# Linear attention and a gated two-layer network in one kernel: key-value products moved from the first layer to the rows of the batch before

## The chip, the cores and the metric

The kernel runs on one core of one Trainium2 chip. The core has TensorE (PE, matrix products into the PSUM banks), VectorE (DVE), ScalarE (ACT), GpSimd (POOL) and SyncE (SP). Each engine runs its own queue of instructions in order; semaphores make one wait for another. SP and POOL are used here mostly to issue DMA transfers. The metric is the device time of one execution in microseconds, lower is better. Times of single instructions come from one execution that was profiled.

## The reference

For 8 batches of 8 heads, 576 positions and a head size of 64, a linear attention without softmax is followed by a root-mean-square norm, and a two-layer network with a gate is applied to the 4608 rows of 512 numbers that come out:

```python
kv = np.einsum('bhsd,bhse->bhde', k, v)
out = np.einsum('bhsd,bhde->bhse', q, kv)
rms = np.sqrt(np.mean(out * out, axis=-1, keepdims=True) + 1e-06)
x = (out / rms * g_norm)            # per batch, then rows of 8 heads x 64
h = x @ w_in                        # 512 -> 2048
g = h * (1.0 / (1.0 + np.exp(-1.702 * h)))
y = g @ w_out                       # 2048 -> 512
```

Inputs and output are float32. The kernel computes in float16 with float32 sums.

## The kernel before

The program is written out by Python code, with the order of every engine's instructions given by hand. The network works on tiles of 512 rows. The first 512 positions of each batch make one tile, and the last 64 positions of all eight batches make a ninth, so the outer loop has steps t = 0 to 8. Step t runs both layers of tile t on TensorE, and between their products it places the attention of batch b = t + 1.

**The two layers.** For t of 1 and over, each layer is computed with seven products of half-size blocks instead of eight. The *first layer* (`hid_seven`, `SevenIn.product`, L559) is a list of 28 products in the string of a `Plan`, each of four TensorE instructions over 256 columns: "21" is product 1 of part 2. A word "kv" in that string is a place without a product, at which the key-value products of the next batch are hung. The copies that hold intermediate results (`snap`, L509) and the gates (L539) go to ScalarE or VectorE as the plan says. The *second layer* (`Seven.run`, L681) is 112 instructions of 256 columns, numbered n = 0 to 111: products 1, 5, 6, 2, 7, 3, 4 with 16 steps each. Other work is hung on a number with `at2(n, ...)` and stands behind the n-th instruction. A `Plan`'s `ready` and `later` say at which places VectorE forms the sums `gS` (L611) that products 5, 6, 7 and 3 read; an entry (4, 8, 1) forms rows 4 to 7 of sum 1. One product of the first layer ("34") is late: it stands behind step 15.

**The attention of batch b** (class `Attention`, batches 2 to 7) has these pieces:

- `load_kv`, `load_q` (L114 to L140): POOL issues the loads of k, v and q of the first 512 positions, and of the rest of 64 positions. There is one buffer for k and one for v (`kraw`, `vbuf`), so a load waits until the products before have read them. There are two for q.
- `kv_all` (L238): for each pair of heads ten small products k'v, 40 in all, into one PSUM tile `kvp`; then four copies (`keep_kv`) move it into `kvd`, of which there are two that alternate by batch.
- `transpose_q` (L273, L275): SP issues transposing DMAs of q.
- `rows` (L313): q times `kvd`, 32 small products for half of the rows; ScalarE squares both halves (`sq`, L323, three buffers).
- `add_up` (L329), `roots` (L338), `turn` (L341): VectorE sums the squares per head, ScalarE takes the inverse root, VectorE multiplies; SP transposes the result with two DMAs into `xT`, which is the next tile of the network.
- `out`, `ss`, `apply` (L287, L358, L374): the same norm for the 64 positions of the rest.

In step t = 2 to 6 (plan `LATER`) the key-value products of batch t + 1 stand in the first layer as its third word, the loads of batch t + 2 behind its 15th, and `rows` behind step 15 of the second layer, both halves at once, right behind the late product. Step t = 1 uses the plan `SECOND`, with "kv" as its 22nd word and `rows` behind step 19. The allocation of a PSUM tile picks a free bank of its pool: `ps_a` and `ps_h` hold three banks each, `ps_o` two.

Of the kernel before, what the change touches and what calls it, by code (L numbers as in the profile page):

```python
# [7 lines left out]
F16 = mybir.dt.float16  # L8
# [4 lines left out]
P = 128  # L13
# [3 lines left out]
def kernel(  # L17
# [10 lines left out]
    nc = tc.nc  # L28

    B, H, S, D = q.shape  # L30
    DM = H * D
    DFF = moe_w_in.shape[1]
    NPAIR = H // 2
    FO = DFF // P
    KO = DM // P
    EPS = 1e-6
    SM = 512
    J = SM // P
# [10 lines left out]
    const = ctx.enter_context(tc.tile_pool(name="const", bufs=1))  # L49
    stage = ctx.enter_context(tc.tile_pool(name="stage", bufs=4))  # L50
    attn = ctx.enter_context(tc.tile_pool(name="attn", bufs=4))
# [18 lines left out]
    ident = const.tile([P, P], F16)  # L70
    ones2 = const.tile([P, P], F16)
    eps_t = const.tile([P, 1], F32)
    g_col = const.tile([P, 1], F32)
    w_in_sb = const.tile([P, KO, DFF], F16)
    w_out_sb = const.tile([P, FO, DM], F16)
# [32 lines left out]
    RW = J * D  # L108
    RS = H * RW

    def load_kv(b, h0=0, h1=H, rest=True):

        for n in "kv":
            nc.gpsimd.dma_start(  # L114
                out=kv_rows[n][:, h0 * RW : h1 * RW].rearrange("p (h x) -> p h x", x=RW),
                in_=srcs[n][b, h0:h1, 0:SM, :].rearrange("h (p j) d -> p h (j d)", j=J),
            )
        for n in "kv" if rest else "":
            nc.gpsimd.dma_start(
                out=kv_rows[n][0:R, RS : RS + H * D].rearrange("p (h d) -> p h d", d=D),  # L120
                in_=srcs[n][b, :, SM:S, :].rearrange("h p d -> p h d"),
            )

    def clear_rest():
        for n in "kv":
            nc.vector.memset(kv_rows[n][R:P, RS : RS + H * D], 0.0)
# [19 lines left out]
    for n in "kqv":  # L146
        if n != "q":
            rows = stage.tile([P, 6, 2 * P], F32, name="qf", tag="qf", bufs=2)
            rows = rows.rearrange("p h x -> p (h x)")[0:PE_]
# [8 lines left out]
        out=ident,  # L158
        in_=ident,
# [42 lines left out]
    xT = {}  # L202
# [8 lines left out]
    class Attention:  # L211
# [3 lines left out]
        def __init__(self, b):  # L215
            self.b, self.kb = b, kvb[b] if b < EARLY else kvd[b % 2]
            self.qT, self.o = {}, {}
            x = xpool.tile([P, KO * SM], F16, name="xT", tag="xT")
            if b < EARLY:
                self.x = xT[b] = x.rearrange("p (c n) -> p c n", c=KO)  # L220
            else:
                self.x = x.rearrange("p (m r) -> p m r", r=P)
                xT[b] = x.rearrange("p (j c r) -> p c j r", j=J, c=KO)
                self.x16 = attn.tile([P, J, DM], F16, name="x16", tag="x16", bufs=1)

        def kv(self, c):
            if c % self.KEEP == 0:
# [35 lines left out]
        def keep_kv(self, c0, c1):  # L263

            for half in range(2):
                to = slice(half * D, (half + 1) * D)
                for hl in range(2):
                    r = slice(hl * D, (hl + 1) * D)
                    copy(self.engine, self.kb[to, c0:c1, half, 1 - hl], self.kvp[r, c0:c1, :])

        def transpose_q(self):
            self.qTd = attn.tile([P, H * J // 2, P], F16, name="qTd", tag="qTd", bufs=1)
# [16 lines left out]
        def out(self, c):  # L289
            pool, tag = (ps_a, "att") if c < NPAIR else self.rest_pool  # L290
            t = pool.tile([P, SM], F32, name="outT", tag=tag)
            if c < NPAIR:
                n = SM
                self.product(t, c)
            else:
                n = NPAIR * R
                for i in range(NPAIR):
                    self.rest_product(t[:, i * R : (i + 1) * R], i)
            t = t[:, 0:n]
            sq = attn.tile([P, SM], F16, name="sq", tag="sq", bufs=3)  # L300
            nc.scalar.activation(sq[:, 0:n], t, AFT.Square)
            self.o[c] = (t, sq, n)

        def rows(self, i):

            t = [
                pool.tile([P, DM], F32, name="outR", tag=tag)
                for pool, tag in ROW_BANKS[i]
            ]
            for h in range(H):  # L310
                for half in range(2):
                    r = slice(half * D, (half + 1) * D)
                    nc.tensor.matmul(  # L313
                        t[half][:, h * D : (h + 1) * D],
                        self.qTd[r, h * (J // 2) + i, :],
                        self.kb[r, h // 2, half, 1 - h % 2, :],
                        start=(h == 0),
                        stop=True,
                        skip_group_check=True,
                    )  # L320
            for half in range(2):
                sq = attn.tile([P, SM], F16, name="sq", tag="sq", bufs=3)
                nc.scalar.activation(sq, t[half], AFT.Square)  # L323
                self.o[2 * i + half] = (t[half], sq)

# [12 lines left out]
            nc.scalar.activation(s4, s4, AFT.Abs_reciprocal_sqrt, bias=eps_t, scale=1.0 / D)  # L338

        def turn(self, j):  # L340
            nc.vector.tensor_mul(  # L341
                self.x16[:, j, :].rearrange("p (h d) -> p h d", d=D),
                self.o[j][0].rearrange("p (h d) -> p h d", d=D),
                self.sum4[:, j, :].unsqueeze(2).to_broadcast([P, H, D]),
            )
            if j % 2:
                nc.sync.dma_start_transpose(
                    out=self.x[:, (j - 1) * KO : (j + 1) * KO, :],
                    in_=self.x16[:, j - 1 : j + 1, :].rearrange("p j n -> p (j n)"),
                )  # L350
# [157 lines left out]
    def copy(engine, to, src):  # L508
        (nc.vector.tensor_copy if engine == "D" else nc.scalar.copy)(to, src)  # L509
# [347 lines left out]
    for hl in range(2):  # L857
        r = slice(hl * D, (hl + 1) * D)
# [34 lines left out]
    for fo in COLS[4:GROUP]:  # L893
# [28 lines left out]
        {'rows': (19, 19), 'add_up': (22, 26, 27, 31), 'table': 26, 'roots': (27, 33), 'turn': (40, 50, 51, 52)},  # L922
    )
    LATER = Plan(
# [4 lines left out]
        {1: 'DAAA', 5: 'AAAD'},  # L929
        "D",  # L930
        "aooa",
        "aahh",
        {15: '34'},
        (0, 1, 6, 11),
        {'rows': (15, 15), 'add_up': (17, 20, 24, 28), 'table': 24, 'roots': (28, 39), 'turn': (35, 38, 46, 48)},
    )
    LAST_TWO = Plan(
# [12 lines left out]
    def plan(t):  # L950
        return SECOND if t < EARLY else LATER if t < B - 1 else LAST_TWO
# [7 lines left out]
    for t in range(NT):  # L959
        b = t + 1  # L960
        u1, u2 = {}, {}

        def at1(i, f, *args):
            u1.setdefault(i, []).append(lambda: f(*args))

        def at2(i, f, *args):
            u2.setdefault(i, []).append(lambda: f(*args))  # L967

        def of(b, name, *args):
            return lambda: getattr(live[b], name)(*args)  # L970

        if t == 0:
# [25 lines left out]
            at2(39, load_kv, 2, 0, H // 2, False)  # L998
            at2(51, clear_rest)
            at2(51, load_kv, 2, H // 2, H)  # L1000

            def first_sum():
# [3 lines left out]
            at2(55, first_sum)  # L1006
        elif b < B:
            todo = plan(t)
            at1(todo.steps.index("kv"), of(b, "kv_all", todo.keep))
            if t == 1:  # L1010
                at1(5, start, b)
                at1(5, of(b, "transpose_q"))
                at1(4, nc.scalar.preload_act_table_set, "gelu_apprx_sigmoid_and_others")
                for n, i in ((1, 8), (2, 11), (3, 16)):
                    at1(i, weight_sum, n, 6, HF)
            if t + 2 < B:
                late = max(15, todo.steps.index("kv") + 1)
                at1(late, load_kv, t + 2)
                at1(late, load_q, t + 2)
                at2(100, start, t + 2)  # L1020
                at2(100, of(t + 2, "transpose_q"))
            at = todo.attn
            at2(at["table"], nc.scalar.preload_act_table_set, "abs_reciprocal_sqrt_and_small")
            for h in range(2):
                at2(at["roots"][h], of(b, "roots", h))
            for j in range(J):
                if j < J // 2:
                    at2(at["rows"][j], of(b, "rows", j))
                for name in ("add_up", "turn"):
                    at2(at[name][j], of(b, name, j))  # L1030
            at2(46, of(b, "out", NPAIR))
            at2(74, of(b, "ss", NPAIR))
            at2(80, of(b, "apply", NPAIR))
            at2(82, nc.scalar.preload_act_table_set, "gelu_apprx_sigmoid_and_others")
        elif t < B:
            for name in ("ss_pool", "rest_pool"):
                at2(16, setattr, live[1], name, (ps_a, "att"))
            at2(16, of(1, "out", NPAIR))
            at2(34, nc.scalar.preload_act_table_set, "abs_reciprocal_sqrt_and_small")
            at2(44, of(1, "ss", NPAIR))  # L1040
            at2(50, of(1, "apply", NPAIR))
            at2(52, nc.scalar.preload_act_table_set, "gelu_apprx_sigmoid_and_others")
# [31 lines left out]
```

## Time and profile before

| | |
|---|---|
| median of 3 runs | 259.46 us (258.91 to 261.26) |
| the profiled execution | 259.37 us |
| its span, first to last instruction | 257.6 us |
| busy: PE, DVE, ACT, POOL | 250.6, 195.0, 174.9, 55.0 us |
| clock granted to TensorE | 1.00 |
| kvp products (L238), 240 instructions | 4.9 us busy |
| copies of kvp (L509, VectorE, 64x256), 24 | 10.1 us busy |
| moved by DMA | 35.33 MB, mean 137 GB/s |

Busy times of one engine overlap those of another, so they don't add up to the span. A row of a timeline gives the start in us from the first instruction, the length, the engine, the line of the kernel, the operation, and "out<-in" with the shape (partitions x elements). Several instructions of one kind that follow each other are one row with "x" and their number. In brackets stands how long the engine was idle ahead of it and what ended the wait.

### The profile page before, as it was taken

The numbers are of one execution on the slowest core, as the hardware profiler recorded it, in microseconds if no ns is written. First come the engines' busy times: TensorE is split into PE (matmuls) and PEld (weight loads), VectorE is DVE, ScalarE is ACT, GpSimd is POOL, SyncE is SP. The second block draws the span as 40 slices with busy tenths as digits, with TensorE's granted clock in tenths as the row PEclk, the third lists the DMA queues.
The fourth block names the chain that finished last, engine by engine and source line by source line (L and its number), as shares of the span: only waits on it lengthen the run. The fifth ranks groups of instructions, "written<-read, shape, count | busy, mean of one in ns | idle before, by whom it ended". The sixth has DMA issues, their size and how long they took to land.

```text
span 257.6 us, 6353 instructions
## 1 busy us (share of the span) xinstructions
PE 250.6 (97%) x2596; PEld 203.3 (79%) x2596; DVE 195.0 (76%) x351; ACT 174.9 (68%) x315; POOL 55.0 (21%) x83
## 2 busy tenths in 40 slices
PE   7889999999999999999999999999999999999993
PEld 2434554788888888888888888888888888888883
DVE  1655677899968896889689968996899687557842
ACT  3477825988749974997499748984798569737820
POOL 8963245117025002500160007000000000000011
PEclk9999999999999999999999999999999999999999
DMA  7999999999989947996799479948600430012005
GB/s 170 200 202 206 204 204 197 230 200 138 161 194 170 215 59 151 154 213 90 172 147 223 62 177 138 229 58 178 159 4 0 93 154 3 0 79 88 3 21 142
DMA packets 68607, 35.33 MB, mean 137 GB/s; under 512 B 37922, under 2 KB 66082, under 8 KB 68322
## 3 DMA queue, kind: packets, MB, share of 16 engines
q0 software_dynamic: 37552, 18.17, 55.1%
q1 hardware_dynamic: 30624, 16.36, 27.9%
q8 instruction: 20, 0.33, 0.5%
q10 hardware_dynamic: 402, 0.39, 0.5%
q14 instruction: 9, 0.07, 0.1%
HBM read 36.70 MB, written 9.44 MB: 179 GB/s over the span
## 4 chain that ended last, share of the span: by engine, by line
PE 92%; POOL 3%; DMA 3%; issue 0%; DVE 0%
PE o L681 38%; PE h L559 38%; PE o L795 5%; PE hT L452 5%; DMA w_in_sb<-in_moe_w_in_dram 3%; PE kvp L238 2%; PE outR L313 1%; POOL kraw L90 1%; POOL qraw L90 1%; PE ss L358 1%; POOL vbuf L90 1%; POOL w_in_sb L171 0%; PE q L433 0%; PE kvp L250 0%; PE outT L283 0%; PE outT L287 0%
## 5 line engine op out<-in xcount | busy, mean ns | idle before, releaser
L539 ACT ACTIVATE gT<-h 128x512 f16<-128x512 f32 x96 | 52.5, 602 | 5.4 <-PE h L559 5.4
L559 PEld LDWEIGHTS <-ws 128*128 128x128 f16 x512 | 50.1, 98 | 5.9
L681 PEld LDWEIGHTS <-gS 128*128 128x128 f16 x512 | 49.4, 98 | 6.2 <-DVE gS L611 0.3
L559 PE MATMUL h<-xS,ws 128*128 128x256 f16 x384 | 52.2, 273 | 0.0
L681 PE MATMUL o<-tw,gS 128*128 128x256 f16 x384 | 46.5, 273 | 0.0
L681 PEld LDWEIGHTS <-gT 128*128 128x128 f16 x384 | 37.5, 98 | 4.3
L559 PEld LDWEIGHTS <-w_in_sb 128*128 128x128 f16 x384 | 37.1, 98 | 4.7
L559 PE MATMUL h<-xT,w_in_sb 128*128 128x256 f16 x224 | 31.9, 273 | 0.0
L681 PE MATMUL o<-w_out_sb,gT 128*128 128x256 f16 x256 | 31.4, 273 | 0.0
L573 DVE TENSOR_TENSOR h<-h,s 128x512 f32<-128x512 f32 x32 | 22.2, 697 | 6.8 <-PE h L559 5.5
L114 POOL DMA_DIRECT2D kraw<-in_k_dram x7 | 6.0, 853 | 91.0 <-PE kvp L238 86.5
L575 DVE TENSOR_TENSOR s<-h,s 128x512 f32<-128x512 f32 x32 | 22.1, 691 | 4.1 <-PE h L559 3.3
L656 DVE TENSOR_TENSOR osb<-o,qf 128x512 f32<-128x512 f32 (+1 forms) x25 | 16.7, 667 | 11.2 <-PE o L681 8.3
L611 DVE TENSOR_TENSOR gS<-gT 128x512 f16<-128x512 f16 (+2 forms) x32 | 21.2, 684 | 0.6 <-ACT gT L539 0.6
L539 ACT ACTIVATE gT<-s 128x512 f16<-128x512 f32 x32 | 19.9, 628 | 2.6 <-DVE s L575 2.6
L714 POOL DMA_DIRECT2D out_dram<-osb x4 | 2.2, 546 | 90.9 <-DVE osb L656 90.9
L559 PE MATMUL h<-xS,w_in_sb 128*128 128x256 f16 x128 | 18.9, 273 | 0.0
L360 ACT ACTIVATE rs<-ss,eps_t 128x512 f32<-128x512 f32 (+1 forms) x16 | 9.2, 581 | 13.7 <-PE ss L358 13.6
L967 ACT ACT_TABLE_LOAD x14 | 18.0, 1283 | 0.2
L648 ACT COPY qf<-o 128x512 f32<-128x512 f32 (+1 forms) x26 | 14.2, 546 | 4.5 <-PE o L681 4.4
L329 DVE TENSOR_REDUCE sum<-sq 128x8 f32<-128x512 f16 x24 | 15.3, 680 | 2.5 <-ACT sq L323 2.5
L509 ACT COPY h<-h 128x512 f32<-128x512 f32 x27 | 15.7, 586 | 2.1 <-PE h L559 2.0
(100 smaller groups left out, 361.9 us busy)
## 6 DMA issues: line engine op xcount, KB each, us to landing
out_dram<-osb SPq DMA_DIRECT2D x8, 512.0 KB, 4.2
kraw<-in_k_dram POOLq DMA_DIRECT2D x5, 512.0 KB, 9.2
vbuf<-in_v_dram POOLq DMA_DIRECT2D x5, 512.0 KB, 12.1
out_dram<-osb SPq DMA_DIRECT2D x2, 1024.0 KB, 4.9
qraw<-in_q_dram POOLq DMA_DIRECT2D x3, 512.0 KB, 13.4
qbuf<-in_q_dram POOLq DMA_DIRECT2D x3, 512.0 KB, 13.3
out_dram<-osb SPq DMA_DIRECT2D x6, 192.0 KB, 5.5
w_in_sb<-in_moe_w_in_dram POOLq DMA_DIRECT2D x2, 512.0 KB, 10.7
```

The costliest lines, as they stand in the source:

```text
L329: nc.vector.tensor_reduce(out=self.sum4[:, j, :], in_=self.o[j][1].rearrange("p (x d) -> p x d", d=D), op=ALU.add, axis=mybir.AxisListType.X,)
L452: nc.tensor.matmul(self.h[fo], w_in_sb[:, ko, fo * P : (fo + 1) * P], self.x[:, ko], start=(ko == 0), stop=(ko == KO - 1),)
L509: (nc.vector.tensor_copy if engine == "D" else nc.scalar.copy)(to, src)
L539: nc.scalar.activation(self.gT[:, to, n * TH : (n + 1) * TH], src, AFT.Gelu_apprx_sigmoid)
L559: nc.tensor.matmul(bank[name][:, a], w, x, start=(p in (1, 5) and a == 0 and k == 0), stop=(k == KH - 1), skip_group_check=True,)
L573: nc.vector.tensor_add(bank["z"], bank["x"], self.s5)
L575: nc.vector.tensor_add(self.s5, bank["x"], self.s5)
L611: op(s[:, n, lo], a, b)
L648: nc.scalar.copy(self.kept[as_][:, m], ps)
L656: nc.vector.tensor_add(o, ps, self.kept[with_][:, m])
L681: nc.tensor.matmul(o, a, w, start=(p in (1, 2, 5) and i == 0 and (mo == 0 or split)), stop=(i == HF - 1), skip_group_check=True,)
L967: u2.setdefault(i, []).append(lambda: f(*args))
```

## The change

1. For t = 1 the products of batch 2 stay in the first layer. Those of batch 3 go to step 95 of the second layer, with the copies on VectorE, ScalarE, VectorE, ScalarE ("DADA"), and the loads of batch 4 follow behind step 96.
2. For t = 2 to 5 the products of batch t + 2 stand behind step 15 of the second layer, right ahead of `rows` of batch t + 1, with the copies on ScalarE, VectorE, ScalarE, VectorE ("ADAD"). So the products of batches 4 to 7 come a step earlier than `rows` of the same batch. The word "kv" leaves the plan `LATER`, whose first products change order.
3. For t = 2 to 4 the load of k of batch t + 3 follows these products. The loads of v, of the rests and of q stand behind step 101, and behind a POOL copy of one element (`mark`) out of `xT[b]`, so that POOL waits there until the transposed rows of batch t + 1 have landed.
4. `x16` is allocated in the first `turn` and no longer when a batch starts; there are four buffers `sq` instead of three.
5. `ss`, `apply` and the table load of the second layer go from steps 74, 80, 82 to 82, 88, 90. In `LATER`, sum (4, 8, 3) goes from step 22 to 29, and the sums `ready` and `xsums` follow the shorter list.

```diff
-    def load_kv(b, h0=0, h1=H, rest=True):
-
-        for n in "kv":
+    def load_kv(b, h0=0, h1=H, rest=True, main="kv"):
+
+        for n in main:
...
+    def after_turn(b):
+
+        nc.gpsimd.tensor_copy(out=mark, in_=xT[b].rearrange("p c j r -> p j c r")[0:1, J - 1, KO - 1, 0:1])
...
-                    copy(self.engine, self.kb[to, c0:c1, half, 1 - hl], self.kvp[r, c0:c1, :])
+                    copy(
+                        self.engine[2 * half + hl],
+                        self.kb[to, c0:c1, half, 1 - hl],
+                        self.kvp[r, c0:c1, :],
+                    )
...
-            sq = attn.tile([P, SM], F16, name="sq", tag="sq", bufs=3)
+            sq = attn.tile([P, SM], F16, name="sq", tag="sq", bufs=4)
...
         def turn(self, j):
+            if j == 0:
+                self.x16 = attn.tile([P, J, DM], F16, name="x16", tag="x16", bufs=1)
...
     LATER = Plan(
-        "21 01 kv 22 05 25 06 11 02 15 26 03 16 12"
+        "21 01 25 22 05 06 11 02 15 26 03 16 12"
         " 07 31 27 13 17 35 36 04 23 24 32 33 14 37",
-        {23: ((0, 4, 0), (0, 4, 1)), 26: ((4, 6, 0),)},
-        {0: ((0, 8, 2),), 16: ((4, 8, 1),), 22: ((4, 8, 3),), 58: ((0, 4, 3),)},
+        {22: ((0, 4, 0), (0, 4, 1)), 25: ((4, 6, 0),)},
+        {0: ((0, 8, 2),), 16: ((4, 8, 1),), 29: ((4, 8, 3),), 58: ((0, 4, 3),)},
...
-        (0, 1, 6, 11),
+        (0, 1, 5, 10),
...
         elif b < B:
             todo = plan(t)
-            at1(todo.steps.index("kv"), of(b, "kv_all", todo.keep))
+            at = todo.attn
             if t == 1:
+                at1(todo.steps.index("kv"), of(b, "kv_all", "DDDD"))
...
+                at1(22, load_kv, 3)
+                at1(22, load_q, 3)
+                at2(95, start, 3)
+                at2(95, of(3, "kv_all", "DADA"))
+                at2(96, load_kv, 4)
+                at2(96, load_q, 4)
+            elif t + 2 < B:
+                at2(at["rows"][0], start, t + 2)
+                at2(at["rows"][0], of(t + 2, "kv_all", "ADAD"))
+                if t + 3 < B:
+                    at2(at["rows"][0], load_kv, t + 3, 0, H, False, "k")
+                    at2(101, after_turn, b)
+                    at2(101, load_kv, t + 3, 0, H, True, "v")
+                    at2(101, load_q, t + 3)
             if t + 2 < B:
-                late = max(15, todo.steps.index("kv") + 1)
-                at1(late, load_kv, t + 2)
-                at1(late, load_q, t + 2)
-                at2(100, start, t + 2)
                 at2(100, of(t + 2, "transpose_q"))
...
-            at2(74, of(b, "ss", NPAIR))
-            at2(80, of(b, "apply", NPAIR))
-            at2(82, nc.scalar.preload_act_table_set, "gelu_apprx_sigmoid_and_others")
+            at2(82, of(b, "ss", NPAIR))
+            at2(88, of(b, "apply", NPAIR))
+            at2(90, nc.scalar.preload_act_table_set, "gelu_apprx_sigmoid_and_others")
```

More of the change, by code (lines that the diff above doesn't have):

```diff
@@ L72 @@
     eps_t = const.tile([P, 1], F32)
+    mark = const.tile([1, 1], F16)
     g_col = const.tile([P, 1], F32)
@@ L223, in __init__ @@
                 xT[b] = x.rearrange("p (j c r) -> p c j r", j=J, c=KO)
-                self.x16 = attn.tile([P, J, DM], F16, name="x16", tag="x16", bufs=1)
         def kv(self, c):
@@ L321, in rows @@
             for half in range(2):
-                sq = attn.tile([P, SM], F16, name="sq", tag="sq", bufs=3)
+                sq = attn.tile([P, SM], F16, name="sq", tag="sq", bufs=4)
                 nc.scalar.activation(sq, t[half], AFT.Square)
@@ L1015 @@
                     at1(i, weight_sum, n, 6, HF)
+                at1(22, load_kv, 3)
[12 more added lines that the diff above has]
+                    at2(101, load_q, t + 3)
             if t + 2 < B:
-                late = max(15, todo.steps.index("kv") + 1)
-                at1(late, load_kv, t + 2)
-                at1(late, load_q, t + 2)
-                at2(100, start, t + 2)
                 at2(100, of(t + 2, "transpose_q"))
-            at = todo.attn
             at2(at["table"], nc.scalar.preload_act_table_set, "abs_reciprocal_sqrt_and_small")
```

## The prediction

> **What bounds the kernel now.** I read the page's head first, then the chain of work that ended last in order of time, then the timelines of the second layer. The page:
>
> ```profile
> span 257.6 us, 6353 instructions
> PE 250.6 (97%) x2596; PEld 203.3 (79%) x2596; DVE 195.0 (76%) x351; ACT 174.9 (68%) x315; POOL 55.0 (21%) x83
> ```
>
> TensorE is busy for 250.6 of 257.6 us ; VectorE has 76%, ScalarE 68%. The profiled execution took 259.37 us, so 1.77 us lie around its span; the median of the runs is 259.46. The chain in order of time (start, length, work) for one step of the loop, t = 3, from the start of its first layer to the start of the next:
>
> ```profile
> 99.69 0.87 PE h L559 x8
> 100.56 0.75 PE kvp L238 x40
> 101.31 11.02 PE h L559 x100
> 112.33 1.75 PE o L681 x16
> 114.08 0.44 PE h L559 x4
> 114.52 0.57 PE outR L313 x32
> 115.09 3.49 PE o L681 x31
> 118.58 0.12 PE outT L287 x4
> 118.70 3.06 PE o L681 x28
> 121.75 0.11 PE ss L358
> 121.86 4.04 PE o L681 x37
> 125.90 0.87 PE h L559 x8
> ```
>
> The step lasts 125.90 - 99.69 = 26.21 us, and every piece is PE: nothing stalls it. A big product takes 4.04/37 = 0.109 us. So nothing is left to be gained from a stall. What the edits can win is the fixed cost of switching shapes: 100 products after kvp took 11.02 instead of 10.92, and 31 after outR took 3.49 instead of 3.38, 0.10 each time. What they can lose is any wait that TensorE does not have now.
>
> **Where the slack is thin.** The timelines of VectorE, ScalarE and TensorE around the second layer of t = 3 (start, length, instruction; in brackets the idle time ahead of it and what ended that):
>
> ```profile
> 112.37 0.69 DVE L575 TENSOR_TENSOR s<-h,s 128x512 f32<-128x512 f32 x1 [0.16 <-PE h L559]
> 114.56 0.69 DVE L611 TENSOR_TENSOR gS<-gS,gT 128x1024 f16<-128x1024 f16 x1
> 115.73 1.28 DVE L329 TENSOR_REDUCE sum<-sq 128x8 f32<-128x512 f16 x2 [0.47 <-ACT sq L323]
> 116.92 0.68 DVE L611 TENSOR_TENSOR gS<-gT,gS 128x1024 f16<-128x1024 f16 x1
> 117.52 1.27 DVE L329 TENSOR_REDUCE sum<-sq 128x8 f32<-128x512 f16 x2
> 118.81 2.48 DVE L341 TENSOR_TENSOR x<-outR,sum 128x512 f16<-128x512 f32 x4
> 121.22 0.68 DVE L611 TENSOR_TENSOR gS<-gT,gS 128x1024 f16<-128x1024 f16 x1
> ...
> 113.10 0.63 ACT L539 ACTIVATE gT<-s 128x512 f16<-128x512 f32 x1 [0.25 <-DVE s L575]
> 114.60 0.60 ACT L539 ACTIVATE gT<-h 128x512 f16<-128x512 f32 x1
> 115.09 2.08 ACT L323 ACTIVATE sq<-outR 128x512 f16<-128x512 f32 x4
> 117.18 1.28 ACT L967 ACT_TABLE_LOAD   x1
> 119.63 0.58 ACT L648 COPY qf<-o 128x512 f32<-128x512 f32 x1
> ...
> 114.45 0.64 PE L313 MATMUL outR<-kvd,qTd 64*128 64x64 f16 x32
> 120.39 1.36 PE L681 MATMUL o<-tw,gS 128*128 128x256 f16 x11
> 122.25 1.91 PE L681 MATMUL o<-w_out_sb,gS 128*128 128x256 f16 x16
> 126.71 0.82 PE L238 MATMUL kvp<-vbuf,kraw 128*64 128x64 f16 x40
> 127.46 0.61 PE L559 MATMUL h<-xT,w_in_sb 128*128 128x256 f16 x4
> ...
> 126.42 0.59 ACT L509 COPY h<-h 128x512 f32<-128x512 f32 x1
> ```
>
> and the groups of instructions by shape (count, then busy us and mean ns of one):
>
> ```profile
> L509 DVE CAST kvd<-kvp 64x256 f16<-64x256 f32 x24 | 10.1, 420 | 0.2
> L648 ACT COPY qf<-o 128x256 f32<-128x256 f32 x4 | 1.5, 370 | 0.8 <-PE o L681 0.8
> ```
>
> The product that begins at 122.25 (step 80 of 112 in `Seven.run`, the 17th after 120.39 without `ss`) reads gS rows 0 to 3 of the fourth sum. VectorE finishes them at 121.22 + 0.68 = 121.90, only 0.35 us ahead. From 114.56 on VectorE runs (4,8,1), two `add_up`, (4,8,3), two `add_up`, four `turn`, and that sum, with one pause, 115.25 to 115.73. Back to back one takes about 0.60 (four turns in 2.48, the last 0.68 to its end). This vector chain is what the change lengthens.
>
> **The change, part by part.**
>
> *Leaving the first layer.* For t = 2 to 6 the products kvp go from the third place of the first layer: 0.75 + 0.10 for the switch back = 0.85 us each off the chain. Batch 3's come back at step 95 of the second layer of t = 1, again between big products: +0.85. Their copies D, A, D, A (some 1.70 us, priced below) run beside the last 16 products of that layer, 16 x 0.109 = 1.75 us, and the first vector sum of the next layer is asked for by its third product, 0.87 us further on. So I cost the copies there at nothing; without that cover they would cost up to their own 1.70, once.
>
> *Entering the second layer, t = 2 to 5 (batches 4 to 7).* The 40 small products stand directly ahead of the 32 of `rows`, so one switch may be saved. On TensorE that is 0.75 at most, and 0.75 - 0.09 = 0.66 if the entry of outR goes too (0.57 less 32 at some 0.015 leaves about 0.09); I take 0.72.
>
> *The copies.* Before, four copies on VectorE, in the first layer, where its queue held slack. Now they go A, D, A, D, and in the order of the built program each waits for the one before on the other engine: the first waits for TensorE, the second for ScalarE's first, the third for VectorE's first, the fourth for ScalarE's second. All four read one tile. Behind the waiting VectorE copies stands (4,8,1) and the whole vector chain; behind ScalarE's second copy stand the four squares. No row shows this copy on ScalarE. The nearest row is L648 with the same 256 elements a lane, 0.370; with 512 it takes 0.58 (119.63 row). I take 0.37, bounds 0.37 to 0.58. On VectorE it is 0.420 by its own row. A hand-over from engine to engine costs 0.04 by the rows above (VectorE ends at 113.06, the ScalarE gate that waits for it starts at 113.10).
>
> The sum for t = 3, the small products starting where `rows` start now, at 114.45, and taking 0.82 to their last result (126.71 row): end 115.27. A to 115.64, D 115.68 to 116.10, A 116.14 to 116.51, D 116.55 to 116.97. So (4,8,1) starts at 116.97, not 114.56: 2.41 late. The pause before `add_up` is gone, since the squares (116.51 to 118.59) now come before they are asked for. Ten operations of 0.60 and one of 0.68 end at 123.65, and step 80 starts at 123.69, not 122.25. Without the chain TensorE would be there at 122.25 + 0.72 - 0.11 = 122.86, as `ss` (0.11) moves from step 74 to behind it, step 82. **A stall of 0.83 us**, in which an earlier one is contained: step 64 (120.39, now 121.11) waits for L648, whose queue is squares to 118.59, table to 119.87, then five short pieces to about 121.6.
>
> Per step, then: +1.44 at step 80, +0.11 for `ss`, -0.85 from the first layer = **+0.70 us**. It does not hang on the 0.72, because the vector chain ends last. Four steps: +2.80.
>
> *Weighed against the skill.* By the waits in the program the copies follow one another. The Trainium skill (PSUM — Partial Sum Buffer, PSUM bank collisions raise a hardware error) says that two engines may work in one bank at once as long as they are in different quadrants of 32 partitions, and these pairs are: one copies partitions 0 to 63, the other 64 to 127. By it the copies would end after two, not four; no run here shows it. That is the first rival below, worked out there from rows.
>
> *Loads.* `load_kv` splits: k right behind the products, v, the rests and q behind a POOL copy (`mark`) that waits until the x transposes have landed. That copy is one element and no row shows one; between nothing and the 0.7 us of a small issue it only moves these loads, which alone stand behind it. Rows of the DMA view for 100 to 113 us (last number: us from issue to landing), its row for the x transposes over the whole span, and two issues from POOL's timeline:
>
> ```profile
> kraw<-in_k_dram POOLq DMA_DIRECT2D x1, 512.0 KB, 10.5
> vbuf<-in_v_dram POOLq DMA_DIRECT2D x1, 512.0 KB, 13.1
> vbuf<-in_v_dram POOLq DMA_DIRECT2D x1, 64.0 KB, 12.4
> xT<-x SPq DMA_TRANSPOSE x12, 3.2
> ...
> 102.47 0.90 POOL L114 DMA_DIRECT2D vbuf<-in_v_dram  x1
> 104.01 0.72 POOL L119 DMA_DIRECT2D vbuf<-in_v_dram  x1
> ```
>
> k is issued near 115.3 and at 10.5 would land at 125.8, beside the x transposes; in that row v and the q transposes ran beside it, now nothing does, so I expect it earlier. The last turn ends at 123.65 - 0.60 = 123.05 instead of 121.29, so the x transposes land near 126.3 (3.2 after issue), ahead of the next first layer at 125.74 + 1.55 = 127.29. Then v and the two rests are issued, 0.9 + 0.7 + 0.7 (POOL's rows), by 128.6. At the 12.4 of its row the last rest lands at 141.0; the next small products want it at 127.29 + 128 x 0.109 = 141.2 (108 big products in the first layer, 16 and 4 in the second). The row has 512 KB more ahead of it than there will be, so I take it as hidden, and keep a miss as a rival. The q transposes move past nothing: they stay at step 100, and q is now there a whole step earlier.
>
> *At nothing:* `x16` allocated later, four sq buffers, `(4,8,3)` from step 22 to 29 (same vector chain), `apply` and the table load eight steps later (next use a layer away). With the new order "21 01 25 22" product 22 starts after one product of 0.44 where 0.85 of kvp stood, at 127.46 - 0.41 = 127.05, and the ScalarE copy it needs ends at 126.42 + 0.59 = 127.01: 0.04 us of slack. This I cost at nothing, and at up to +0.1 a step in the range.
>
> **Rivals.** *Nothing stalls (faster):* if copies ran in pairs, 115.27 + 0.74 or 0.84 = 116.11, the vector chain would end at 122.79, before 122.86. Then each step gains 0.85 - 0.72 = 0.13, four 0.52: **258.8**. For it: the saved switch is seen in the rows. Against it: the waits. *The v loads are late (slower):* v's last rest lands when v's own 13.1 row says, 128.6 + 13.1 = 141.7, and the small products at step 15 wait 0.5 us; it decides as soon as landing takes over 12.6. Three steps (batches 5 to 7) give 1.5 more, **263.7**. For it: a queue that took 12.4 to 13.1 where it was full. Against: it will be less full. *ScalarE's copy costs what 512 elements cost:* 2 x 0.21 more in each chain, 1.7 in all, **263.9**. *The products do not move:* excluded, the built order has them ahead of outR.
>
> **How the numbers follow.** 259.37 + 2.80 = 262.2 us, on the profile's own time; the median of before is 0.09 higher. Chances: forecast (261.2 to 263.2) 0.60, nothing or little stalls (258.6 to 261.2) 0.18, late loads 0.12, dearer copies or added small waits 0.10. Range 259.6 to 264.8: it leaves out the low half of the second case and the tails of the last two. One percent, about what a measurement of this kernel can tell, is 2.6 us: slower needs over 262.05, which is all of the last two cases and half of the first, 0.52; faster by over 2.6 us has no source, since all switches together are worth less than 1 us, 0.03; within, 0.45.
>
> **What would show it.** Right: VectorE copies of kvp alternate with ScalarE's, some 1.7 us from first to last; VectorE idle ahead of both; TensorE waits for gS (L611) at step 80 and for ScalarE's qf near step 64, 0.5 to 1 us a step for t = 2 to 5; the step grows from 26.21 to about 26.91. Wrong: no gap in PE there, or a DMA named ahead of kvp. The prediction would be wrong most cheaply if VectorE's operations overlap more than 0.60 apart once they need not wait.

## The result, and the profile after

The changed kernel took 263.38 us, the median of 6 runs (262.65 to 264.47); the kernel before, timed beside it, took 259.42 us (6 runs, 258.91 to 261.26). The ratio is 1.0156, with a 95% interval from 1.0134 to 1.0179: **slower by 1.6%, about 4.0 us**. The prediction was 262.2 us in a range of 259.6 to 264.8, so the sign and the place were right and the size was 1.2 us too small. 263.38 lies just above the band of 261.2 to 263.2 us that the forecast had given a chance of 0.60.

The execution that was profiled took 264.47 us, the longest of the six. The head of its page:

```profile
span 262.7 us, 6343 instructions
PE 253.3 (96%) x2596; PEld 203.9 (78%) x2596; DVE 190.9 (73%) x341; ACT 180.1 (69%) x325; POOL 56.2 (21%) x86
```

By the page TensorE is busy 2.7 us longer than before, and the other 2.4 of the 5.1 us by which the span grew are idle. The page counts a product as busy up to an end that is modelled, so a part of the new waits, worked out below, stands in the busy time. The chain of work that ended last, in order of time, for t = 3 of the changed kernel (start, length, work), which answers to the twelve rows shown of before:

```profile
102.92 11.80 PE h L569 x108
...
116.91 0.78 PE kvp L242 x40
...
117.71 0.38 ACT kvd L519
...
118.96 2.07 ACT sq L331 x4
...
125.61 0.61 DVE gS L621
126.26 0.50 PE o L691 x3
...
130.04 11.80 PE h L569 x108
```

Before, all twelve pieces of this step were PE. Now the chain leaves TensorE at the end of the small products, 117.69, and comes back only at step 80, 126.26: in between the step hangs on the copies, the squares, the load of a function table by ScalarE (`table`), the turns and the last vector sum. The first layer lost its break (108 products in 11.80, no switch of shape), as foreseen. (The 32 products of `rows` that follow the small products are both halves of the rows, 16 each.) The step lasts 130.04 - 102.92 = 27.12 us instead of 26.21.

From the starts of the first layers in the two chains, the lengths of the steps are as follows. The chain of after leaves TensorE at the start of t = 2, so this one start is taken from TensorE's timeline: 75.26, plus the 0.16 by which the chain gives such a start later, is 75.42.

| step | before | after | difference | what stands there |
|---|---|---|---|---|
| until the first layer of t = 1 | 47.00 | 48.09 | +1.09 | nothing that was changed |
| t = 1 | 26.47 | 27.33 | +0.86 | batch 3's products at step 95 |
| t = 2 | 26.22 | 27.50 | +1.28 | batch 4's, and a wait for their load |
| t = 3 | 26.21 | 27.12 | +0.91 | batch 5's |
| t = 4 | 26.22 | 27.12 | +0.90 | batch 6's |
| t = 5 | 26.22 | 27.10 | +0.88 | batch 7's |
| t = 6 | 26.21 | 25.37 | -0.84 | no products any more |

The edited steps give +3.99 us, near the 3.96 between the medians. The +1.09 ahead of them belongs to this one execution, which lies 1.09 above the median. The row of the first 17 us, which no edit touches, in the table by stretches of the changed kernel and then of the kernel before (the last three numbers are the granted clock, the DMA share and GB/s):

```profile
0.00:17.00 17.00, 14.59 (x131) 6.21 (x132) 6.51 (x18) 6.35 (x9) 14.72 (x28) 0.90 1.09 184
```

```profile
0.00:17.00 17.00, 13.89 (x134) 6.06 (x135) 7.29 (x20) 8.01 (x11) 13.97 (x27) 1.00 1.12 188
```

The clock was 0.90 there, against 1.00 before. In the profiles of e1 to e5, e7 and e8 below, whose programs are the same up to there, it was 1.00 and the first layer of t = 1 began at 46.90 to 47.38 us; in e6 and e9 it was 0.91 and 0.90, and the layer began at 48.77 and 48.34. So the lengths of the steps can be compared, the two spans can't.

Where TensorE waits in an edited step shows in its timelines, t = 3 (idle time ahead and what ended it in brackets):

```profile
116.84 0.82 PE L242 MATMUL kvp<-vbuf,kraw 128*64 128x64 f16 x40
124.12 1.91 PE L691 MATMUL o<-tw,gS 128*128 128x256 f16 x16 [0.43 <-ACT qf L658]
126.26 0.50 PE L691 MATMUL o<-w_out_sb,gS 128*128 128x256 f16 x3 [0.23 <-DVE gS L621]
...
117.71 0.37 ACT L519 CAST kvd<-kvp 64x256 f16<-64x256 f32 x1
118.11 0.42 DVE L519 CAST kvd<-kvp 64x256 f16<-64x256 f32 x1 [1.19 <-ACT kvd L519]
118.57 0.36 ACT L519 CAST kvd<-kvp 64x256 f16<-64x256 f32 x1 [0.49 <-DVE kvd L519]
118.97 0.43 DVE L519 CAST kvd<-kvp 64x256 f16<-64x256 f32 x1 [0.43 <-ACT kvd L519]
119.42 0.69 DVE L621 TENSOR_TENSOR gS<-gS,gT 128x1024 f16<-128x1024 f16 x1
120.03 2.46 DVE L337 TENSOR_REDUCE sum<-sq 128x8 f32<-128x512 f16 x4
122.41 0.68 DVE L621 TENSOR_TENSOR gS<-gT,gS 128x1024 f16<-128x1024 f16 x1
123.12 2.48 DVE L351 TENSOR_TENSOR x<-outR,sum 128x512 f16<-128x512 f32 x4
125.52 0.68 DVE L621 TENSOR_TENSOR gS<-gT,gS 128x1024 f16<-128x1024 f16 x1
```

The four copies alternate, each with the copy before it named as what ended the wait, and (4,8,1) starts 1.76 us after the products' end at 117.66. From the last copy on VectorE runs without a pause, to 125.52 + 0.68 = 126.20; so its own queue is as long as the way over ScalarE that the chain names. TensorE then waits twice: at step 64 for ScalarE's copy qf, which stands behind the squares and the table load, and at step 80 for VectorE's last sum. The brackets say 0.43 and 0.23. They count from the end that is modelled for the last product, which is 273 ns long where the next follows 109 ns after its start, so TensorE loses 0.16 more at each: 0.59 and 0.39, together 0.98. Less the 0.10 of the saved switch this is the +0.88 to +0.91 of the table.

In t = 2 something else comes on top. The timeline of TensorE there:

```profile
89.34 0.32 PE L242 MATMUL kvp<-vbuf,kraw 128*64 128x64 f16 x8
89.85 0.69 PE L242 MATMUL kvp<-vbuf,kraw 128*64 128x64 f16 x32 [0.20 <-DMA vbuf<-in_v_dram]
```

and the chain of the changed kernel at that place:

```profile
76.28 13.53 DMA vbuf<-in_v_dram
```

After 8 of the 40 products TensorE waits for the last 64 KB of v, issued at 76.28 and landed 13.53 us later. Without it the other 32 would have started at 89.34 + 8 x 0.75/40 = 89.49, so TensorE lost 0.36 us, about the excess of 27.50 over 27.12. For batches 5 to 7 the same pieces landed 9.6 to 11.0 us after issue, and nothing waited.

### The profile page after: what moved, and what is told of

Its sections match the earlier page's. It is cut to its first block, busy times and chain, and to the rows that moved or that the text cites. A ratio compares the mean times of both kernels' runs of the same rounds, so it can differ in the third digit from the quotient of the medians.

```text
span 262.7 us, 6343 instructions
## 1 busy us (share of the span) xinstructions
PE 253.3 (96%) x2596; PEld 203.9 (78%) x2596; DVE 190.9 (73%) x341; ACT 180.1 (69%) x325; POOL 56.2 (21%) x86
## 4 chain that ended last, share of the span: by engine, by line
PE 78%; DMA 7%; DVE 5%; ACT 4%; POOL 3%; issue 1%; DVEq 0%
PE h L569 33%; PE o L691 30%; PE o L805 5%; PE hT L462 5%; DMA vbuf<-in_v_dram 5%; DVE x L351 3%; DMA w_in_sb<-in_moe_w_in_dram 2%; PE kvp L242 2%; ACT sq L331 2%; ACT L977 1%; DVE gS L621 1%; PE outR L321 1%; POOL qraw L91 1%; PE ss L368 1%; POOL kraw L91 1%
## 5 line engine op out<-in xcount | busy, mean ns | idle before, releaser
L569 PE MATMUL h<-xS,ws 128*128 128x256 f16 x384 | 53.0, 273 | 0.0
L691 PE MATMUL o<-tw,gS 128*128 128x256 f16 x384 | 45.8, 273 | 1.7 <-ACT qf L658 1.7
L691 PE MATMUL o<-w_out_sb,gS 128*128 128x256 f16 x128 | 16.0, 273 | 0.9 <-DVE gS L621 0.9
## 6 DMA issues: line engine op xcount, KB each, us to landing
qbuf<-in_q_dram POOLq DMA_DIRECT2D x3, 512.0 KB, 13.1
```

The source lines that it names most:

```text
L569: nc.tensor.matmul(bank[name][:, a], w, x, start=(p in (1, 5) and a == 0 and k == 0), stop=(k == KH - 1), skip_group_check=True,)
L691: nc.tensor.matmul(o, a, w, start=(p in (1, 2, 5) and i == 0 and (mo == 0 or split)), stop=(i == HF - 1), skip_group_check=True,)
```

## The experiments

**The theory:** what costs is that four copies of kvp stand in the queues of VectorE and ScalarE ahead of the vector sums and the squares; which engine makes them matters little. **The rivals:** that the hand-overs between the engines cost (then copies on one engine are cheap); that the products cost anywhere in the second layer; that the loads or the later `ss` do it. The first four kernels ran on one chip (before there: 259.82 us, 13 runs), e5 to e8 on another (259.56, 23 runs), e9 by itself (259.31, 11 runs).

### e1 and e2: the four copies on one engine

```diff
-                at2(at["rows"][0], of(t + 2, "kv_all", "ADAD"))
+                at2(at["rows"][0], of(t + 2, "kv_all", "DDDD"))   # e1; "AAAA" in e2
```

> The changed kernel, but the four copies of kvp for batches 4 to 7 all on VectorE ('DDDD'), so no copy waits for the other engine. Theory (what counts is how long VectorE is held ahead of its sums): four copies of 0.43 are 1.72 us, as long as the alternating chain of 1.76, so (4, 8, 1) starts at the same distance from the products, the steps t = 3 to 5 stay at 27.1 us (within 0.1) and the time at that of the changed kernel; only the wait at step 64 for ScalarE's qf goes, and its share moves to step 80. Rival (the hand-overs between the engines are the cost): the steps fall to 26.2 to 26.5 us and the kernel is 2.5 to 3.5 us faster than the changed one.

> The changed kernel, but the four copies for batches 4 to 7 all on ScalarE ('AAAA'). Theory: VectorE starts (4, 8, 1) at once, but ScalarE's squares still wait for four copies, about 1.3 to 1.5 us, so the qf that step 64 needs is as late as in the changed kernel; the stall of 0.59 us before step 64 stays (up to 0.8 if the copies don't overlap), that before step 80 goes, and a step takes 26.7 to 26.9 us. In all 1 to 1.7 us faster than the changed kernel, still slower than the kernel before. Rival (hand-overs are the cost): 26.2 to 26.5 us a step, as in the run with VectorE alone.

Measured, four runs each: e1 264.56 us, ratio to before 1.0199 (1.0169 to 1.0230); e2 262.75 us, 1.0125 (1.0098 to 1.0153). The first layers of t = 3 and 4 in the chain of e1:

```profile
101.41 11.80 PE h L569 x108
128.58 11.80 PE h L569 x108
```

and its timelines between them:

```profile
116.20 1.73 DVE L519 CAST kvd<-kvp 64x256 f16<-64x256 f32 x4 [0.79 <-PE kvp L242]
117.96 0.69 DVE L621 TENSOR_TENSOR gS<-gS,gT 128x1024 f16<-128x1024 f16 x1
124.80 0.50 PE L691 MATMUL o<-w_out_sb,gS 128*128 128x256 f16 x3 [0.73 <-DVE gS L621]
```

The same two views of e2:

```profile
101.75 11.80 PE h L569 x108
128.74 11.80 PE h L569 x108
```

```profile
116.54 1.50 ACT L519 CAST kvd<-kvp 64x256 f16<-64x256 f32 x4
118.06 2.06 ACT L331 ACTIVATE sq<-outR 128x512 f16<-128x512 f32 x4
118.69 2.46 DVE L337 TENSOR_REDUCE sum<-sq 128x8 f32<-128x512 f16 x4 [2.22 <-ACT sq L331]
123.23 1.91 PE L691 MATMUL o<-tw,gS 128*128 128x256 f16 x16 [0.70 <-ACT qf L658]
```

With all copies on VectorE they last 1.73 us, the vector chain starts 1.81 us after the products' end (116.15) and the step is 27.17 us, with nearly the whole wait at step 80. With all on ScalarE they last 1.50, VectorE is free but waits 2.22 us for the first square, the whole wait is at step 64, and the step is 26.99. So the rival of the hand-over falls: without any hand-over the step is 0.05 us longer or 0.13 shorter than the 27.12 of the alternating order. There are two chains from the copies to TensorE, one through VectorE to step 80, one through ScalarE to step 64, and each order loads one of them or half of both. e2 came out 0.1 to 0.3 us a step above what I expected: its squares start 1.57 us after the products' end (116.49), where they start 1.30 after it in the changed kernel, and the wait at step 64 is 0.86 us (0.70 + 0.16) instead of 0.59. The median of e1 is 1.2 us above the changed kernel's, which I had not expected. The steps of its profile don't show that (t = 2 to 5 last 27.16 to 27.17 us, and that execution took 263.19 us); where its other three runs lost time stays open.

### e3: two of the four copies left out

```diff
-            for half in range(2):
+            for half in range(1 if self.b > 3 else 2):
```

> The changed kernel with two of the four copies left out for batches 4 to 7 (one on ScalarE, one on VectorE; the second half of kvd keeps older values, so the rows from batch 4 on are computed from them). Theory: both chains are 0.88 us shorter, and the losses before steps 64 and 80, 0.59 and 0.39 us a step, are covered by that in full or up to 0.1: steps t = 3 to 5 of 26.1 to 26.3 us. Rival (the loss comes from the products' place or from the loads, not from the copies): steps stay near 27.1.

Measured: 259.23 us, one run. The chain of e3, and its timelines:

```profile
100.67 11.80 PE h L569 x108
126.80 11.80 PE h L569 x108
```

```profile
122.29 0.68 DVE L621 TENSOR_TENSOR gS<-gT,gS 128x1024 f16<-128x1024 f16 x1
123.02 0.50 PE L691 MATMUL o<-w_out_sb,gS 128*128 128x256 f16 x3
```

The step is 26.13 us, 0.08 below before, and no wait is left at steps 64 and 80. The last sum ends at 122.97 and step 80 starts at 123.02: one copy on each engine is what just fits. Two copies more and the step is 0.99 us longer.

### e4: the products at step 95

```diff
-                at2(at["rows"][0], start, t + 2)
-                at2(at["rows"][0], of(t + 2, "kv_all", "ADAD"))
+                at2(95, start, t + 2)
+                at2(95, of(t + 2, "kv_all", "DADA"))
                 if t + 3 < B:
-                    at2(at["rows"][0], load_kv, t + 3, 0, H, False, "k")
+                    at2(96, load_kv, t + 3, 0, H, False, "k")
```

> The changed kernel, but the products of batches 4 to 7 at step 95 with the copies D, A, D, A, as the change does for batch 3; the load of k behind step 96. Everything else as changed: loads split, ss later, new order of the first layer. Theory: the copies run beside the last product, ahead of no sum that is soon needed, so no stall; each step costs 26.2 us (the 0.85 us that the first layer saves are paid at step 95), and the kernel comes to 259.3 to 260.0, within 0.3% of the kernel before. Rival (a batch a step early, or the split loads and the marker, cost by themselves): steps of 26.6 us and more.

Measured: 259.68 us in 10 runs, ratio 0.9991 (0.9974 to 1.0007), no difference from before. In its chain the first layers of t = 3 and 4 start here:

```profile
100.50 11.80 PE h L569 x108
126.73 11.80 PE h L569 x108
```

The step is 26.23 us. The same products and the same four copies, late in the second layer where no sum or square stands behind them, cost nothing but the switch of shape. So neither the move into the second layer nor the alternation costs, but the place ahead of `rows`.

### e6 and e7: the split of the loads, and `ss`

```diff
 # e6
-                    at2(at["rows"][0], load_kv, t + 3, 0, H, False, "k")
-                    at2(101, after_turn, b)
-                    at2(101, load_kv, t + 3, 0, H, True, "v")
-                    at2(101, load_q, t + 3)
+                    at2(at["rows"][0], load_kv, t + 3)
+                    at2(at["rows"][0], load_q, t + 3)
 # e7
-            at2(82, of(b, "ss", NPAIR))
-            at2(88, of(b, "apply", NPAIR))
-            at2(90, nc.scalar.preload_act_table_set, "gelu_apprx_sigmoid_and_others")
+            at2(74, of(b, "ss", NPAIR))
+            at2(80, of(b, "apply", NPAIR))
+            at2(82, nc.scalar.preload_act_table_set, "gelu_apprx_sigmoid_and_others")
```

> The changed kernel with the loads not split and without the marker copy: k, v, rests and q of batches 5 to 7 are all issued behind the products at step 15 of the second layer of t = 2 to 4. Tells what the split is for. Theory (1.1 MB then move beside the x transposes at the end of the same layer): the x transposes take longer than the 3.1 to 3.2 us of the changed kernel in t = 2 to 4, 4 to 8 us; the next first layer starts with products that need x and waits for them, so t = 3 to 5 grow from 27.12 by 1 to 4 us each, 266 to 275 us in all. Rival (transposes are not slowed by loads): the steps stay at 27.1, 263 us, and v's landing is no longer near its deadline.

> The changed kernel with the last sum of squares, the scaling and the table load of the second layer back at steps 74, 80 and 82 (from 82, 88 and 90). The prediction put +0.11 us a step on this move, because TensorE's sum of squares then came behind the wait at step 80 and not in it. Theory: t = 3 to 5 go from 27.12 to 27.01 us, 0.45 us less in all. Rival (the sum of squares waits itself for the late ScalarE square at step 74, or VectorE's scaling comes ahead of the fourth sum): no gain or a longer step, 27.1 to 27.5.

Measured, one run each: e6 279.84 us, e7 263.13 us. The chain of e6 where it leaves TensorE at the end of t = 2, then the row of TensorE's timeline at that place, and a row by stretches behind the wait (the last three numbers: clock, DMA share, GB/s):

```profile
97.62 8.06 DMA xT<-x
105.72 13.63 PE h L569 x108
```

```profile
105.72 1.67 PE L569 MATMUL h<-xT,w_in_sb 128*128 128x256 f16 x8 [2.50 <-DMA xT<-x]
```

```profile
107.00:109.00 2.00, 2.00 (x11) 1.40 (x10) 1.05 (x3) 0.73 (x2) 0.00 (x0) 0.50 1.25 283
```

The transposes of x take 8.06 us instead of 3.1 to 3.2 while k, v and q move, and TensorE idles 2.50, 3.01 and 2.89 us by the brackets for them at the end of t = 2, 3 and 4, with the 0.16 of the modelled end 8.9 us in all. That is the first half of the price; the second I had not expected: behind each of these pauses the granted clock fell to 0.50, and the first layer took 13.63 to 14.80 us instead of 11.80, by its excess an estimated 4 to 6 us at half the clock, 6.7 us lost in all. Without these 6.7 the total would lie inside the 266 to 275 us that I gave. The split with the `mark` copy (0.18 to 0.44 us in the changed kernel) is thus what keeps the change from costing about 15 us more (279.84 against 264.47, two profiled executions that both start at the low clock); it does its work.

e7's step is 27.04 us (t = 3, from the starts 101.76 and 128.80 in its chain), 0.08 less than 27.12. `ss` now waits itself, 0.17 us in the bracket, for the last turn (L351), so not the whole 0.11 comes back.

### e5, e8 and e9: the second half copied by GpSimd

```diff
                 to = slice(half * D, (half + 1) * D)
+                if half and self.b > 3:
+                    break
                 for hl in range(2):
...
+        def second_half(self):
+            nc.gpsimd.tensor_copy(out=self.kb[D:P, :, 1], in_=self.kb[0:D, :, 0])
...
                     at2(at["rows"][0], load_kv, t + 3, 0, H, False, "k")
+                at2(at["rows"][0], of(t + 2, "second_half"))
+                if t + 3 < B:
                     at2(101, after_turn, b)
```

In e8, and differently in e9, batch 4's q load is moved as well:

```diff
-                at2(96, load_q, 4)
...
                 at1(22, load_q, 3)
+                at1(22, load_q, 4)      # e9
...
             elif t + 2 < B:
+                if t == 2:
+                    at1(15, load_q, 4)   # e8
```

> For batches 4 to 7 the products stay ahead of the rows; ScalarE and VectorE make only the first two of the four copies from PSUM, and the other two, which write the same numbers to partitions 64 to 127, become one copy of 64 x 1024 elements by GpSimd from SBUF to SBUF, behind the k load's issue. All work is done. Theory (what costs is the four copies standing in the queues of VectorE and ScalarE, and nothing else of the move): steps like those of the two-copies kernel, 26.13 us (26.10 to 26.20) in t = 3, 4 and 5, 0.10 below the kernel before's 26.21 to 26.22, no gap of TensorE at steps 64 and 80, and 259.0 to 259.5 us where the kernel before has 259.4 to 259.8. Rival (the second writes are needed sooner, or a GpSimd copy slows what VectorE does beside it): GpSimd's copy shows long, VectorE's back-to-back pitch grows beyond 0.60 to 0.62 us, and TensorE waits for gS at step 80 again: 26.4 to 27.1 per step, 260.5 to 263.

> The previous kernel of this call, with batch 4's q load issued 15 products into the first layer of t = 2 and not behind its k, v and rests in the second layer of t = 1. In the profiles so far the last of batch 4's rests (64 KB of v) landed 12.5 to 13.5 us after its issue, with 512 KB of q issued behind it, and the products of batch 4 waited for it twice in four profiles, by about 0.4 us (t = 2 lasted 27.50 instead of 27.12 in the changed kernel). Theory (q behind it shares the DMA engines and stretches it): that rest lands in 8 to 11 us, no wait for a DMA ahead of the products of batch 4, t = 2 as long as t = 3. Rival (what is ahead of it, k and v, sets its landing): 12.5 to 13.5 us as before, and a wait in some executions. Time: as the previous kernel, or up to 0.4 us less; 258.8 to 259.5.

> The kernel with two copies and GpSimd's copy (e5), with batch 4's q load issued right behind batch 3's q load in the first layer of t = 1. In e8 the load had only been written further down; GpSimd's queue waits for nothing between the two places, so the order of every queue stayed as in e5, and the last 64 KB of v landed after 13.1 us as before. Here the order does change: no q follows batch 4's v. Theory (512 KB of q behind it shares the DMA engines): the 64 KB of v land 8 to 11.5 us after issue, 1.5 us or more ahead of the products of batch 4. Rival (k and v ahead of it set its landing): 12.5 to 13.5 us as before. Time either way 258.9 to 259.5, steps of 26.13 in t = 2 and 3; the time is not what tells the two apart.

Measured: e5 259.62 us in 12 runs, ratio 1.0018 (1.0000 to 1.0036); e8 259.28 us in 12 runs, 0.9982 (0.9966 to 0.9998); e9 262.96 us in 6 runs (260.87 to 265.42), 1.0100 (1.0069 to 1.0131). GpSimd's copy is of 64 x 512 elements, not the 64 x 1024 that I wrote. The chain of e5, and its timelines:

```profile
100.84 11.80 PE h L574 x108
126.97 11.80 PE h L574 x108
```

```profile
116.78 0.74 POOL L282 COPY kvd<-kvd 64x512 f16<-64x512 f16 x1
116.97 2.45 DVE L342 TENSOR_REDUCE sum<-sq 128x8 f32<-128x512 f16 x4
122.46 0.68 DVE L626 TENSOR_TENSOR gS<-gT,gS 128x1024 f16<-128x1024 f16 x1
123.19 0.50 PE L696 MATMUL o<-w_out_sb,gS 128*128 128x256 f16 x3
```

With all the work done, the step is 26.13 us again in t = 2 and 3, as in e3, and 26.19 and 26.17 in t = 4 and 5 (first layers from 126.97 on at 153.16 and 179.33); in t = 3 no wait is left. GpSimd's copy takes 0.74 us, and the four `add_up` beside it take 2.45 us, where the changed kernel has 2.46: it doesn't lengthen them. This takes back the whole loss of the changed kernel. It is no settled gain over the kernel before: 26.22 to 26.13, 26.21 to 26.13, 26.22 to 26.19 and 26.22 to 26.17 make 0.25 us, 0.1%. e8 turned out to be e5 once more: GpSimd's queue waits for nothing between the old and the new place of that load, so the instructions of all queues have the same order. Its timing and e5's differ by 0.34 us, and their intervals don't overlap; e5 is 0.1 above the range I gave, e8 inside it. Two timings of one program can be that far apart, so 0.2% can't be told here.

e9 was meant to show what delays batch 4's v. Its 64 KB landed 13.1 us after issue although no q followed them. But the earlier q (11.5 us from issue to landing) now ran beside the transposes of x at the end of t = 1, as the chain of e9 shows:

```profile
70.44 7.97 DMA xT<-x
```

They took 7.97 us where they take 4.2 in e5, TensorE waited for them, and the kernel was slower, 3.5 us above the time I expected. In the profiled execution this wait cost 2.6 us: from the start of t = 1 to that of t = 3 it needs 104.39 - 48.34 = 56.05 us, e5 53.47. That is e6's mechanism at another place; the rest is the late start at the low clock in this execution, and no run separates the two in the others. Since q's own transposes were late too and ran beside v, the run doesn't tell whether q or what is ahead of v sets its landing. It stays open.

## Why the prediction was right and where it was off

- **Leaving the first layer, -0.85 a step; batch 3's move at no more than the move.** This was right: t = 1 grew by 0.86, t = 6 shrank by 0.84, and e4 shows four copies at step 95 hidden.
- **The copies in a row, on the vector chain, a stall at step 80 and one at step 64.** The rows show each part as forecast: ScalarE's copy (0.36 to 0.37, taken as 0.37), the alternation, and the two waits. The rival that the copies run in pairs didn't come: each copy starts 0.02 to 0.04 us after the end of the one before. That speaks of the waits in this program, not of the chip. The rule of the Trainium skill (PSUM — Partial Sum Buffer, PSUM bank collisions raise a hardware error), that two engines may work in one bank at once in different quadrants, is neither borne out nor refuted: in no run do two copies of one kvp tile overlap on two engines.
- **+0.70 a step.** This was too small by about 0.2. The term that was mis-sized is the vector chain from the products' end to step 80, 1.70 + 6.68 + 0.04 = 8.42 us. It measured 1.76 + 6.78 + 0.06 = 8.60. What the sum lacked is 0.05 from TensorE to the first copy (it started that copy at the very end of the products), 0.11 because the first turn doesn't overlap the operation ahead of it (it starts 0.71 after that operation's start, where I set 0.60 for all ten; the rows of before had it already, 117.52 + 1.27 = 118.79 and the turn at 118.81), and 0.02 at the end. Four steps: 0.8 of the missing 1.2 us.
- **`ss` behind the wait, +0.11.** The size was near: e7 took back 0.07 to 0.08.
- **Loads "taken as hidden".** For batches 5 to 7 this was right: k landed 5.7 to 6.0 us after issue, the last rest of v 9.6 to 11.0. The rival "the v loads are late" I placed at those batches; it came at batch 4, whose load isn't split and whose products moved from the first layer of t = 3 to step 15 of t = 2. There TensorE would have used the piece 89.49 - 76.28 = 13.2 us after its issue. It landed after 13.53, and t = 2 is 0.38 us longer for it; in e2 after 13.51, with 0.33 us lost; in e3 after 13.2, where the 40 products take 0.90 instead of 0.82 us; in e8 after 13.1, and nothing waits. So the wait is a matter of tenths of a us in the landing, and one profile doesn't tell in how many executions of the changed kernel it comes. That I didn't take batch 4's deadline through is the other 0.4 us.
- **The marker at nothing, between 0 and 0.7.** This was right: it took 0.18 to 0.44 us, and nothing behind it was late. The 0.04 us of slack of product 22 in the new order "21 01 25 22" held: the first layer runs 108 products without a gap.
- **The profile's own time as the base.** The sum 259.37 + 3.99 = 263.36 meets the median 263.38, while the profiled execution of after was 1.09 above it, in its first 47 us. That the median lies so near to the 263.7 of the rival of late loads is chance: the rival had three waits of 0.5 us at batches 5 to 7, and none of them came.

## What to carry to other kernels

Before small products are moved next to others of their shape to save a switch (0.10 us here), count what evicts them: each copy takes a place in the queue of an engine whose next instruction may be the one with the thinnest slack, and it pushes everything behind it, not only its own reader. If a copy's reader is far away, put it where nothing urgent stands behind it (e4), or on an engine with an empty queue, by way of a copy in SBUF where the data must be written twice (e5). And take each load that has a new reader through its deadline batch by batch, the first one too, and keep large loads away from transposing DMAs that TensorE waits for.

## What the runs showed of the hardware that was not expected

- Each pause of TensorE of 2.5 to 3.0 us (e6, three of them) was followed by a granted clock of 0.50, worth 1.8 to 3.0 us more in the next first layer. In the changed kernel, which pauses 0.98 us a step in two pieces, it was 1.00 from 17 us on, and in e9 two pauses of 1.51 and 1.08 us, 0.9 us apart, left it at 1.00. The Trainium skill (TensorE: Matmul & The Clock Gate, HAM oscillation — how this bites in real kernels) sets the bound at idle gaps over about 3.4 us. Here a shorter gap was enough: the bracket of 2.50 in e6 is 2.66 us with the 0.16 from the modelled end. Whether the pauses of 0.59 and 0.39 us that stand 4 to 6 us ahead of it count too, no run shows.
- A transpose of x took 3.1 to 3.2 us from issue to landing with no load beside it, and about 8 us beside loads (the two of a step 7.7 to 8.1 on average in e6, 7.9 in e9).
- A GpSimd copy of 64 x 512 elements of float16 from partitions 0 to 63 to partitions 64 to 127 took 0.74 to 0.79 us, without a longer VectorE operation beside it.
- Four copies of kvp took 1.73 us on VectorE, 1.50 on ScalarE and 1.69 in turn on both (117.71 to 118.97 + 0.43 = 119.40): the two engines, each waiting for the other, were no faster than VectorE alone and slower than ScalarE alone.
